# A power's second copy from a DMA to VectorE, three constant loads put back in SyncE's queue, and fewer waits at the program's end

## The chip, the core and the metric

The kernel runs on one core of one Trainium2 chip. The metric is the device time of one execution in microseconds (us), the median of several runs.

## What is computed

The reference mixes two branches over a sequence of 2048 tokens with 512 features, by a gate g of each token:

```python
g = _sigmoid((x * gate_w).sum(-1, keepdims=True))
a = _A_ref(x, A_wq, A_wk, A_wv, A_wo, A_beta)
b = _B_ref(x, B_A_re, B_A_im, B_B_re, B_B_im, B_C_re, B_C_im, B_log_dt, B_Dskip)
return g * a + (1 - g) * b
```

Branch A is causal attention with 32 heads of 16 features, within 4 segments of 512 tokens, plus a read of a memory that collects the earlier segments' keys and values. Branch B is a state space model (S4): from A, B, C and dt it forms a convolution kernel of length 2048 for each of the 512 features,

```python
P = jnp.exp(logdA[:, :, None] * l[None, None, :])
K = jnp.einsum('dn,dnl,dn->dl', Cc, P, dB).real
```

and convolves x with it through Fourier transforms, plus x * Dskip.

## The kernel before

The program is recorded as about 1800 operations, each with an engine, what it reads and writes, and a tag. A table of numbers (ORDER, L375 to L465) gives the sequence in which they are put into the engines' programs, and the buffers that they take; an operation with a number that stands further back is issued later on its engine. Engines run their own programs in order. emit (L267) adds the semaphores: an operation waits only for those earlier operations that its engine does not already know to be done, and this knowledge (know) is passed on through the waits. Each DMA gets a semaphore of its own from a ring of 120.

All DMAs are issued by SyncE (SP), one after the other: loads of inputs and constants, transposes of x, copies from SBUF to SBUF (sb<-sb), stores to the scratch tensors scr_Z and scr_O and loads from them, and 8 stores of the output.

The stages overlap. TensorE (PE) transposes, projects, and multiplies scores; ScalarE (ACT) takes the exponentials of the scores (L1190, L1237) and most evictions from PSUM (L229); VectorE (DVE) builds the tables of the state space kernel, normalises, and applies masks. What the change touches:

- ssm_powers (L840 to L865). For each half h of the features and k from 0 to 9 a complex power z to the 2^k is made by squaring (L850 to L852). A tile pw then holds it in bf16 in four blocks: L857 writes the real and imaginary part (evac of pwc), L862 the negated imaginary part into block 3, and a DMA (L864) copies block 0 into block 1. "Power (3,0)" is k = 3, h = 0. Its copies for k = 2 are not made.
- tables (L1316). For each quarter c it copies powers 0 to 3 into the table F (L1366, which runs as L230 on VectorE), and then multiplies the tables by later powers (L1346, L1349, L1355, L1358). Its fourth copy in quarter 0 reads power (3,0) and waits for the DMA of L864.
- x_level1 (L908). Each of 16 blocks xl1.0 to xl1.15 is multiplied by W1 in two halves, evicted into one of two buffers zs, and stored to scr_Z by a DMA. The next block but one must wait for that store before its eviction.
- Three constant loads: mask01 (32 KB; used by L1249 from 154.5 us on), ones (0.5 KB; used by the product "diag" ahead of L896, at 58.0 us) and sel (6 KB; used in gate_rows, L965, first at 154.3 us).
- The end of SyncE's program (L339 to L342), where it waits for the last count of each of the 120 DMA semaphores. The program's close behind it (L1603) is a barrier of all engines.

Of the kernel before, what the change touches and what calls it, by code (L numbers as in the profile page):

```python
# [98 lines left out]
class Sched:  # L99
# [167 lines left out]
    def emit(self):  # L267
# [43 lines left out]
        cum = {}  # L311
        for e, lst in self.prog.items():
            n = 0
# [10 lines left out]
        def make(e):  # L324
            def run(eng):
                for o in self.prog[e]:
                    need = {}
                    for d in o.waits:
                        s, v = tok(d)
                        if id(s) not in need or need[id(s)][1] < v:  # L330
                            need[id(s)] = (s, v)
                    for s, v in need.values():
                        eng.wait_ge(s, v)
                    ins = o.fn(eng)
                    if o.isdma:
                        ins.then_inc(dsem[o.sem[1]], 16)
                    elif o.inc:
                        ins.then_inc(sems[e], 1)
                if e == "SP":  # L339
                    for k in range(len(dsem)):  # L340
                        if dcnt[k]:
                            eng.wait_ge(dsem[k], 16 * dcnt[k])  # L342
# [21 lines left out]
PW, PWS = (1.0, 8.0), 0.6  # L364
# [16 lines left out]
211a 187/0 212 129/4 1247/0 65 6/0 108 20 127/1 200 128 119 190 1248a 399/0 5/0 183 267a 1036v/0 98v/4 142v/5 213/1/0  # L381
141/6 214a 120 21 139/1 223a 228/0/0/0 1252/2/0 201 229 627/5 628 208/0 1253a 1257/0 140 1040v/0 1039v 1250a 216/3
217a 224 268 1044 225 1037v 1251 1038v 230 842/1 843 130v/6 271/2/1/1 413/1 256/0/0 1042/0 257 1045 151/2 152/7 1254/3
131 1041 153 132 258 231 311/0/2/2 143 1043 89/3 272 233/0/1 234 165/2 227 188 235 1255a 226 154v/7 269/1/1 238/0/2
239 1049 166v/8 312a 144 202/0 1050 270a 155 90 8/0 1237/3/1 156 1046 273 236/0 240 1239/1 1240a 237 241 99/1 1238a
1256 167 242/0/3 168 203/0 243 244 274 1051 1263/2/0 1264a 1047/0 1052 1265/1 101/3 1266a 163/2 357/3/2 287/0/1 288
1053 245 209/0 1048 100 246 1241 416/2 1278/1 289 417a 247/1 1056/0 358a 232/1/0 275 1054 276/0 250/0/3 251 252 400/2
401 1268/3/1 248 164 1270/1 249/0 175a/9 314/2/0 315a 253/0 254 1269a 283/0/3 284 1061 255 259 1055 1271a 1267 4/0 285
1260/2/0 1261a 1272 1258/3 176 177 1057 1259a 278/0/2 279 280 1062 1262 260 261/2 1273/1/1 1275/2 1276a 313 354/3/3/1
355a 316/2/0/0 1274a 1277 1063 301/0/0 1058 262 302 317 1059/0 281/3 263 264 303 403/0 1286/1/0 1287a 282 286 290 402  # L390
291 359/0/1/1 1060 360 319 318 1065 1066/0 295/0/2 292/3 1294/2/1 1295a 296 297 28/0 1067 320/1 361 1296/2 362 363
1068 1069/0 338/0/1 339 1299/0 293 1064 191/0 109/0 1070 1297a 364 1298 192/0 340 1071/2/0 1075/1 1076 1077 204 111/4
110 121/3 294/1 1079/0 1080 1081a 123/0 1072 1078a 205 1073 1074a 1083/0 1086v/0 1088a 1284/3 1285a 1090v/0 122 298/0
356 1087v 299 300 1094 1092/0 1089v 1095 136a/4 330/0/2 331 332 1085 135/6 112v/2 1091 304 1288 133/1 1279/1/1 472/2/1
473a 113 114 1093 305 321/0/3 1099 306/4 1084 1096 322 323 134 145/2 1100 1097/0 1082 405/3/1/0 406a 341/2 342 307
344/0/0 345 1281/3 346 1101 1280a 476/0 308 309 1098 1282a 1283 1102 420/0 1106/0 421a 326/0/1 327 426/1/0/0 146/7 328
1103 1307/3/0 427 1308a 147 157/0 324/0 325 366/0/3 367 368 343 1105 428 408/3/0 1104 80a/0 329 1107 333 334 335/5
# [137 lines left out]
def build_graph(nc, es, A_x, A_wq, A_wk, A_wv, A_wo, A_beta, B_A_re, B_A_im, B_B_re, B_B_im,  # L535
# [304 lines left out]
    def ssm_powers(Zs):  # L840
        Zc = list(Zs)
        for k in range(10):
            for h in range(2):
# [16 lines left out]
                if k == 2:  # L860
                    continue
                op("DVE", ("V4", 256), lambda e, pw=pw: e.tensor_scalar(  # L862
                    ap(pw, 384, [[512, 2], [1, 128]]), ap(pw, 256, [[512, 2], [1, 128]]), -1.0, None, ALU.mult), r=[pw], pw=[pw], key=PW[h] + PWS * k + 0.35)
# [785 lines left out]
```

## Time and profile before

| What | Value |
|---|---|
| Runs of the kernel | 290.23 us median of 3 (289.74, 290.23, 293.19) |
| The profiled execution: span from first to last instruction | 287.5 us |
| Its time outside the span | not recorded; the runs' median is 2.7 us above the span |
| Busy: PE, DVE, ACT | 253.1, 265.0, 254.6 us |
| Mean granted TensorE clock | 0.987 |
| HBM traffic over the span | 104 GB/s |
| Last ACT instruction (L232) ends | 283.0 us |
| Output stores, issue to landing | 8, median 2.1 us |

The profile is of one execution. A row of a timeline gives the start in us from the span's beginning, the length, the engine, line, operation and operands, a count, and in brackets the idle time ahead of it with what ended it; "SPq" rows are DMAs that SyncE issues, and their length is that of the issue. A row of a line ("L225 ... x2: a/b/c, s to e") gives the shortest, median and longest duration in ns, and the first and last start; the landing line under it is the time from issue until the data are there. A row of windows gives the stretch, its length, the busy time of PE, PEld, DVE, ACT and POOL with the number of instructions, the granted clock, the share of the DMA engines, and GB/s.

### The profile page before, as it was taken

What the parts mean: (1) busy time and instruction counts of PE and PEld (TensorE: products, weight loads), DVE (VectorE), ACT (ScalarE), POOL (GpSimd) and SP (SyncE); (2) the same over time, 40 slices, a digit from 0 to 9 for tenths busy, and PEclk for the clock granted to TensorE, in tenths of its full rate; (3) what the DMA queues carried; (4) which work ended last, traced back from release to release, by engine and by line L of the source; (5) the groups of instructions that cost most, each with busy time, mean ns of one, the idle gap of its engine ahead of it and who ended that gap; (6) DMA issues with size and microseconds to landing.
All of it is one profiled execution on the core that took longest, in us unless ns stands there. A gap on an engine that the chain in (4) does not pass through costs nothing.

```text
span 287.5 us, 9336 instructions
## 1 busy us (share of the span) xinstructions
PE 253.1 (88%) x3896; PEld 158.7 (55%) x3947; DVE 265.0 (92%) x617; ACT 254.6 (89%) x320; POOL 5.0 (2%) x10
## 2 busy tenths in 40 slices
PE   5767888787898989979999989999999999999992
PEld 2424454564556546756766657665555454555661
DVE  3998999999999999979999999999999999997782
ACT  5998999999999999989989999999999999983212
POOL 5000000000000000000000000000000000000000
PEclk9999899999999999979999999999999999999999
DMA  6996762421125256914643388585776795894224
GB/s 164 270 223 143 184 203 84 130 87 42 41 47 134 63 141 205 226 32 97 188 132 102 90 252 244 166 232 161 234 215 168 207 229 160 243 186 102 72 109 182
DMA packets 60187, 44.49 MB, mean 155 GB/s; under 512 B 36209, under 2 KB 53490, under 8 KB 60146
## 3 DMA queue, kind: packets, MB, share of 16 engines
q1 hardware_dynamic: 60146, 43.90, 57.0%
q8 instruction: 31, 0.51, 0.8%
q14 instruction: 10, 0.08, 0.1%
HBM read 22.09 MB, written 7.86 MB: 104 GB/s over the span
## 4 chain that ended last, share of the span: by engine, by line
ACT 35%; PE 28%; DVE 26%; issue 5%; DMA 3%; SPq 0%; DVEq 0%; ACTq 0%
PE psum L706 28%; ACT sb L1237 10%; ACT sb L229 10%; ACT sb L1190 8%; DVE sb L1346 7%; DVE sb L1355 3%; ACT sb L850 3%; DVE sb L230 2%; DMA sb<-sb 2%; DVE sb L1349 2%; DVE sb L1487 2%; DVE sb L1358 2%; DVE sb L1249 1%; DVE sb L1154 1%; ACT sb L1021 1%
## 5 line engine op out<-in xcount | busy, mean ns | idle before, releaser
L706 PE MATMUL psum<-sb 128*128 128x17 bf16 (+17 forms) x3808 | 247.4, 229 | 23.5 <-ACT sb L1190 7.4
L706 PEld LDWEIGHTS psum<-sb 128*128 128x128 bf16 (+6 forms) x3859 | 153.5, 102 | 115.5 <-issue 20.7
L229 ACT ACTIVATE sb<-psum 128x512 bf16<-128x512 f32 (+4 forms) x155 | 87.7, 624 | 7.6 <-PE psum L706 6.4
L1237 ACT ACTIVATE sb<-psum 128x2048 bf16<-128x2048 f32 x40 | 76.0, 1899 | 2.1 <-PE psum L706 1.7
L1190 ACT ACTIVATE sb<-psum 128x2048 bf16<-128x2048 f32 (+1 forms) x40 | 70.1, 1751 | 2.8 <-PE psum L706 2.7
L1346 DVE TENSOR_TENSOR sb<-sb 128x4096 bf16<-128x4096 bf16 (+3 forms) x24 | 37.7, 1569 | 0.0
L230 DVE CAST sb<-psum 128x512 bf16<-128x512 f32 (+1 forms) x49 | 29.9, 626 | 1.1 <-PE psum L706 0.9
L1355 DVE TENSOR_TENSOR sb<-sb 128x512 bf16<-128x512 bf16 (+1 forms) x48 | 25.0, 537 | 0.1
L1249 DVE TENSOR_TENSOR sb<-sb 128x1024 bf16<-128x1024 bf16 (+1 forms) x40 | 22.6, 577 | 0.2
L1487 DVE TENSOR_TENSOR sb<-sb 128x1024 bf16<-128x1024 bf16 x32 | 21.6, 685 | 0.9 <-ACT sb L229 0.5
L1349 DVE TENSOR_TENSOR sb<-sb 128x2048 bf16<-128x2048 bf16 (+3 forms) x24 | 20.7, 861 | 0.0
L232 ACT ACTIVATE sb<-psum,sb 128x512 bf16<-128x512 f32 x6 | 4.0, 687 | 12.3 <-PE psum L706 12.3
L1154 DVE TENSOR_TENSOR sb<-psum,sb 128x256 bf16<-128x256 f32 x32 | 13.3, 417 | 0.3
L1358 DVE TENSOR_TENSOR sb<-sb 128x512 bf16<-128x512 bf16 (+1 forms) x24 | 12.9, 536 | 0.0
L850 ACT ACTIVATE sb<-sb 128x512 f32<-128x512 f32 x18 | 11.8, 660 | 0.0
L1151 DVE RECIPROCAL sb<-psum 128x16 f32<-128x16 f32 x32 | 7.9, 252 | 1.8 <-PE psum L706 1.7
L1291 DVE TENSOR_TENSOR sb<-psum,sb 128x512 bf16<-128x512 f32 x12 | 8.2, 687 | 0.2
L858 ACT ACTIVATE sb<-sb 128x512 bf16<-128x512 f32 x12 | 8.0, 683 | 0.0
L1072 ACT ACTIVATE sb<-sb 128x512 bf16<-128x512 bf16 x12 | 8.0, 663 | 0.0
L1021 ACT ACTIVATE sb<-psum 128x512 bf16<-128x512 bf16 x12 | 7.8, 646 | 0.0
L852 DVE SCALAR_TENSOR_TENSOR sb<-sb 128x256 f32<-128x256 f32 x18 | 7.5, 424 | 0.0
L851 DVE TENSOR_TENSOR sb<-sb 128x256 f32<-128x256 f32 x18 | 7.5, 423 | 0.0
(78 smaller groups left out, 122.3 us busy)
## 6 DMA issues: line engine op xcount, KB each, us to landing
sb<-sb SPq DMA_DIRECT2D x64, 128.0 KB, 3.2
sb<-c_DN SPq DMA_DIRECT2D x32, 224.0 KB, 3.0
scr_Z<-sb SPq DMA_DIRECT2D x16, 256.0 KB, 3.2
sb<-scr_Z SPq DMA_DIRECT2D x16, 256.0 KB, 3.6
sb<-in_A_x_dram SPq DMA_DIRECT2D x5, 512.0 KB, 4.6
sb<-c_DN SPq DMA_DIRECT2D x16, 160.0 KB, 3.3
out_dram<-sb SPq DMA_DIRECT2D x8, 256.0 KB, 2.1
scr_O<-sb SPq DMA_DIRECT2D x12, 128.0 KB, 2.7
```

The costliest lines, as they stand in the source:

```text
L229: fa = lambda e: e.activation(dst(), src(), ACT.Copy)
L230: fd = lambda e: e.tensor_copy(dst(), src())
L706: mm = lambda e, o_, l, r_, st, sp, **kw: e.matmul(o_, lhsT=l, rhs=r_, start=st, stop=sp, skip_group_check=True, **kw)
L850: op("ACT", ("As", 512), lambda e, sq=sq, Z=Z: e.activation(ap(sq, n=512), ap(Z, n=512), ACT.Square), r=[Z], w=[sq], key=PW[h] + PWS * k)
L1190: o = op("ACT", ("Ax", 4 * n), lambda e: e.activation(ap(pT, dims=[[512, 4], [1, n]]), ap(P, dims=[[512, 4], [1, n]]), ACT.Exp, scale=0.25 ...
L1237: o = op("ACT", ("Ax", 2048), lambda e, P=P, pT=pT: e.activation(ap(pT, n=2048), ap(P, n=2048), ACT.Exp, scale=0.25), r=[P], w=[pT])
L1249: op("DVE", ("V2", 128 * nb), lambda e, pT=pT, dims=dims: e.tensor_tensor(ap(pT, dims=dims + [[1, 128]]), ap(pT, dims=dims + [[1, 128]]), ...
L1346: op("DVE", ("V2n1" if n == 1 else "V2", 512 * n), lambda e: e.tensor_tensor(ap(tile, 2 * dst, [[2 * (sp - dst), 2], [2 * ne, 128], [1, 2 ...
L1349: op("DVE", ("V2n1" if n == 1 else "V2", 256 * n), lambda e: e.tensor_tensor(D_(), D_(), ap(tile, 2 * sp + ne * 128, [[-ne * 128, 2], [2 * ...
L1355: op("DVE", ("V2x" if sstep > 2 else "V2", 256 * n), lambda e, half=half: e.tensor_tensor(run(t2, n, 0, 1) if half else run(tile, ne, dst, ...
L1358: op("DVE", ("V2", 256 * n), lambda e: e.tensor_tensor(D_(), D_(), ap(t2, n * 128, [[-n * 128, 2], [2 * n, 64], [1, 2 * n]]), ALU.add), r= ...
L1487: op("DVE", ("V2", 1024), lambda e, Y=Y, XAB=XAB, K3=K3, Ke=Ke, xo=xo, u=u: e.tensor_tensor(ap(Y, dims=[[512, 2], [1, 512]]), ap(XAB, xo, ...
```

## The change

Three things are changed.

1. For power (3,0) alone VectorE copies block 0 into block 1, and the DMA that did it is gone. The program has 256 DMAs in place of 257, and the later ones take the semaphore before theirs in the ring.
2. In ORDER the numbers 2/0 (mask01), 6/0 (ones) and 5/0 (sel) stand further back. The numbers themselves keep their meaning, and all others keep their order.
3. At the end of SyncE's program only those DMAs are waited for that no other wait covers. The list is made from the back: a DMA whose count is not yet known to SyncE is put on it, and all that it knows counts as known from then on.

```diff
+        know = last["SP"]
+        tail = []
+        for d in reversed(self.order):
+            if d.isdma and know.get(d.sem, 0) < d.val:
+                tail.insert(0, d)
+                for kk, vv in d.know.items():
+                    if know.get(kk, 0) < vv:
+                        know[kk] = vv
...
                 if e == "SP":
-                    for k in range(len(dsem)):
-                        if dcnt[k]:
-                            eng.wait_ge(dsem[k], 16 * dcnt[k])
+                    for d in tail:
+                        eng.wait_ge(*tok(d))
...
-87 88 106a/2 1242/0 219a 1243a 1245a 104/7 105 115/1 185/0 206/6 107 117/0 91/1 2/0 116 207/0 1246 118a/3 210/1/1/1
+87 88 106a/2 1242/0 219a 1243a 1245a 104/7 105 115/1 185/0 206/6 107 117/0 91/1 116 207/0 1246 118a/3 210/1/1/1 211a
...
                 op("DVE", ("V4", 256), lambda e, pw=pw: e.tensor_scalar(
                     ap(pw, 384, [[512, 2], [1, 128]]), ap(pw, 256, [[512, 2], [1, 128]]), -1.0, None, ALU.mult), r=[pw], pw=[pw], key=PW[h] + PWS * k + 0.35)
+                if (k, h) == (3, 0):
+                    op("DVE", ("V4", 256), lambda e, pw=pw: e.tensor_copy(ap(pw, 128, [[512, 2], [1, 128]]), ap(pw, 0, [[512, 2], [1, 128]])),
+                       r=[pw], pw=[pw], key=PW[h] + PWS * k + 0.4)
+                    continue
                 S.dma(lambda pw=pw: ap(pw, 128, [[512, 2], [1, 128]]), lambda pw=pw: ap(pw, 0, [[512, 2], [1, 128]]), 65536,
                       r=[pw], pw=[pw], key=PW[h] + PWS * k + 0.4)
```

In the rows of the changed program below, line numbers are its own: 7 more than in the profile between L343 and L863, 11 more from L864 on.

SyncE's queue from the second transpose of x on, before. The sb<-sb 128x2x128 copies are second copies of powers: (1,0), then (3,0), then (4,0).

```order
L743 DMA_TRANSPOSE sb<-in_A_x_dram 128x4x512
L225 DMA sb<-sb 128x2x128 [waits q_DVE]
L225 DMA sb<-c_mask01 128x128
L225 DMA scr_Z<-sb 128x2x512 [waits q_ACT]
L225 DMA sb<-c_ones 128x2
L225 DMA sb<-sb 128x2x128 [waits q_DVE]
L743 DMA_TRANSPOSE sb<-in_A_x_dram 128x4x512
L225 DMA sb<-c_sel 128x24
L225 DMA sb<-sb 128x2x128 [waits q_DVE]
L225 DMA sb<-in_A_x_dram 128x2048
```

The same stretch of SyncE's queue now:

```order
L750 DMA_TRANSPOSE sb<-in_A_x_dram 128x4x512
L225 DMA sb<-sb 128x2x128 [waits q_DVE]
L225 DMA scr_Z<-sb 128x2x512 [waits q_ACT]
L750 DMA_TRANSPOSE sb<-in_A_x_dram 128x4x512
L225 DMA sb<-sb 128x2x128 [waits q_DVE]
L225 DMA sb<-in_A_x_dram 128x2048
```

Four DMAs are gone from this stretch: the three loads and the copy of power (3,0); the copies that are left are those of (1,0) and (4,0).

Further back in SyncE's queue, now, around the store of the first attention output to scr_O and the load of Dskip:

```order
L225 DMA sb<-sb 128x2x128 [waits q_DVE]
L225 DMA scr_Z<-sb 128x2x512 [waits q_ACT] x2
L225 DMA sb<-c_mask01 128x128
L225 DMA scr_O<-sb 128x4x128 [waits q_DVE]
L225 DMA sb<-c_sel 128x24
L225 DMA sb<-in_B_Dskip_dram 128x4x1
L225 DMA sb<-in_A_x_dram 128x2048
```

Mask01 and sel have come in here; the other rows stood in this order before. Ones stands between the two, behind the store of xl1.3 and ahead of the copy of power (8,0).

VectorE's program now, from power (3,0)'s negation (its first row) to behind the new copy, which is the row of L872:

```order
L869 TENSOR_SCALAR sb<-sb 128x2x128 [waits q_ACT]
L859 SCALAR_TENSOR_TENSOR sb<-sb 128x256 [waits q_DVE]
L859 SCALAR_TENSOR_TENSOR sb<-sb 128x256
L858 TENSOR_TENSOR sb<-sb 128x256 [waits q_ACT]
L961 TENSOR_SCALAR sb<-psum 128x4 [waits q_PE]
L889 TENSOR_TENSOR sb<-sb 128x512 [waits q_DVE]
L1074 TENSOR_SCALAR sb<-sb 128x512 [waits d19,q_ACT]
L859 SCALAR_TENSOR_TENSOR sb<-sb 128x256 [waits q_DVE]
L872 COPY sb<-sb 128x2x128
L940 TENSOR_SCALAR sb<-sb 128x32
L858 TENSOR_TENSOR sb<-sb 128x256 [waits q_ACT]
L869 TENSOR_SCALAR sb<-sb 128x2x128
```

The copy is the only new row, and it waits for nothing. Further on in the same program, the copies into table F, before:

```order
L230 COPY sb<-sb 128x128x2 [waits q_DVE]
L230 COPY sb<-sb 128x128x2 [waits d25]
L1063 TENSOR_SCALAR sb<-sb 128x512
L1346 TENSOR_TENSOR sb<-sb 128x2x128x2 [waits q_DVE]
L230 COPY sb<-sb 128x128x2 [waits d21]
L230 COPY sb<-sb 128x128x2
```

Now:

```order
L230 COPY sb<-sb 128x128x2 [waits q_DVE]
L230 COPY sb<-sb 128x128x2
L1074 TENSOR_SCALAR sb<-sb 128x512
L1357 TENSOR_TENSOR sb<-sb 128x2x128x2 [waits q_DVE]
L230 COPY sb<-sb 128x128x2 [waits d21]
L230 COPY sb<-sb 128x128x2
```

The second row, which reads power (3,0), no longer waits for a DMA (d25 was the semaphore of its copy).

At the end SyncE waited for all 120 semaphores, in 60 instructions with two semaphores each. Now it waits for six, d13, d14, d12, d15, d11 and d10: those of the last six stores of the output.

More of the change, by code (lines that the diff above doesn't have):

```diff
@@ L379 @@
 189/2 7/0 76 1244/5/0 181/4 1249/4/1 77/3 95/0 22/0 199/0 78/5 96/6 97 103/1 626/0 182/3 86v/1 1/0 184/0 841/0 79 221a
-87 88 106a/2 1242/0 219a 1243a 1245a 104/7 105 115/1 185/0 206/6 107 117/0 91/1 2/0 116 207/0 1246 118a/3 210/1/1/1
-211a 187/0 212 129/4 1247/0 65 6/0 108 20 127/1 200 128 119 190 1248a 399/0 5/0 183 267a 1036v/0 98v/4 142v/5 213/1/0
-141/6 214a 120 21 139/1 223a 228/0/0/0 1252/2/0 201 229 627/5 628 208/0 1253a 1257/0 140 1040v/0 1039v 1250a 216/3
-217a 224 268 1044 225 1037v 1251 1038v 230 842/1 843 130v/6 271/2/1/1 413/1 256/0/0 1042/0 257 1045 151/2 152/7 1254/3
@@ L384 @@
[L384 to L388, printed above, removed]
@@ L389 @@
-1260/2/0 1261a 1272 1258/3 176 177 1057 1259a 278/0/2 279 280 1062 1262 260 261/2 1273/1/1 1275/2 1276a 313 354/3/3/1
[L390 to L397, printed above, removed]
+87 88 106a/2 1242/0 219a 1243a 1245a 104/7 105 115/1 185/0 206/6 107 117/0 91/1 116 207/0 1246 118a/3 210/1/1/1 211a
@@ new lines @@
+187/0 212 129/4 1247/0 65 108 20 127/1 200 128 119 190 1248a 399/0 183 267a 1036v/0 98v/4 142v/5 213/1/0 141/6 214a
+120 21 139/1 223a 228/0/0/0 1252/2/0 201 229 627/5 628 208/0 1253a 1257/0 140 1040v/0 1039v 1250a 216/3 217a 224 268
+1044 225 1037v 1251 1038v 230 842/1 843 130v/6 271/2/1/1 413/1 256/0/0 1042/0 257 1045 151/2 152/7 1254/3 131 1041 153
+132 258 231 311/0/2/2 143 1043 89/3 272 233/0/1 234 165/2 227 188 235 1255a 226 154v/7 269/1/1 238/0/2 239 1049 166v/8
+312a 144 202/0 1050 270a 155 90 8/0 1237/3/1 156 1046 273 236/0 240 1239/1 1240a 237 241 99/1 1238a 1256 6/0 167
@@ new lines @@
+242/0/3 168 203/0 243 244 274 1051 1263/2/0 1264a 1047/0 1052 1265/1 101/3 1266a 163/2 357/3/2 287/0/1 288 1053 245
+209/0 1048 100 246 1241 416/2 1278/1 289 417a 247/1 1056/0 358a 232/1/0 275 1054 276/0 250/0/3 251 252 400/2 401
+1268/3/1 248 164 1270/1 249/0 175a/9 314/2/0 315a 253/0 254 1269a 283/0/3 284 1061 255 259 1055 1271a 1267 4/0 285
+1260/2/0 1261a 1272 1258/3 176 177 1057 1259a 278/0/2 279 280 1062 1262 260 261/2 1273/1/1 1275/2 1276a 313 354/3/3/1
+355a 316/2/0/0 1274a 1277 2/0 1063 301/0/0 1058 262 302 317 1059/0 281/3 263 264 5/0 303 403/0 1286/1/0 1287a 282 286
@@ new lines @@
+290 402 291 359/0/1/1 1060 360 319 318 1065 1066/0 295/0/2 292/3 1294/2/1 1295a 296 297 28/0 1067 320/1 361 1296/2 362
+363 1068 1069/0 338/0/1 339 1299/0 293 1064 191/0 109/0 1070 1297a 364 1298 192/0 340 1071/2/0 1075/1 1076 1077 204
+111/4 110 121/3 294/1 1079/0 1080 1081a 123/0 1072 1078a 205 1073 1074a 1083/0 1086v/0 1088a 1284/3 1285a 1090v/0 122
+298/0 356 1087v 299 300 1094 1092/0 1089v 1095 136a/4 330/0/2 331 332 1085 135/6 112v/2 1091 304 1288 133/1 1279/1/1
+472/2/1 473a 113 114 1093 305 321/0/3 1099 306/4 1084 1096 322 323 134 145/2 1100 1097/0 1082 405/3/1/0 406a 341/2 342
@@ L398 @@
+307 344/0/0 345 1281/3 346 1101 1280a 476/0 308 309 1098 1282a 1283 1102 420/0 1106/0 421a 326/0/1 327 426/1/0/0 146/7
+328 1103 1307/3/0 427 1308a 147 157/0 324/0 325 366/0/3 367 368 343 1105 428 408/3/0 1104 80a/0 329 1107 333 334 335/5
 1108 375/0/1 376 347 160a/3 377 348 1109/0 349/0 418/1 371/0/2 372 419a 409a 1111 124a/1 373 1110 469/1/0/2 1302/3/1
```

## The prediction

> **What bounds the kernel now.** I read the page first, then the chain that ended last, then the timelines of the engines around the two places that the change touches (20 to 31 us, and the end), and last the rows of single transfers.
>
> The page's head, its busy times and the chain's shares by engine:
>
> ```profile
> span 287.5 us, 9336 instructions
> PE 253.1 (88%) x3896; PEld 158.7 (55%) x3947; DVE 265.0 (92%) x617; ACT 254.6 (89%) x320; POOL 5.0 (2%) x10
> ACT 35%; PE 28%; DVE 26%; issue 5%; DMA 3%; SPq 0%; DVEq 0%; ACTq 0%
> ```
>
> No engine is the bound by itself: three are busy for 88 to 92% of the span and share the chain. A stall that holds two of them at once is therefore likely to reach the end, and work that is taken off one of them alone is not. The chain holds one such stall early; these are its pieces from 22 to 31 us (start, length, what):
>
> ```profile
> 22.87 3.02 DMA sb<-sb
> ...
> 25.92 0.30 DVE sb L230
> ...
> 27.63 2.99 PE psum L706 x16
> ...
> 30.64 1.88 ACT sb L1190
> ```
>
> The transfer at 22.87 is the second copy of power (3,0): the vector engine's L230 behind it starts when it lands. What each engine sees of it, first VectorE (start, length, what, and in brackets the idle time before it with its releaser):
>
> ```profile
> 18.79 0.23 DVE L862 TENSOR_SCALAR sb<-sb 128x256 bf16<-128x256 bf16 x1
> ...
> 21.65 0.22 DVE L862 TENSOR_SCALAR sb<-sb 128x256 bf16<-128x256 bf16 x1
> 21.79 0.42 DVE L885 SCALAR_TENSOR_TENSOR sb<-sb 128x256 bf16<-128x256 f32 x1
> ...
> 25.92 0.30 DVE L230 COPY sb<-sb 128x256 bf16<-128x256 bf16 x1 [1.43 <-DMA sb<-sb]
> ```
>
> L862 at 18.79 is the negation that completes power (3,0), so its copy could have been issued at about 19.0. It was issued at 22.87, because SyncE's queue stood in the way:
>
> ```profile
> 20.47 0.61 SPq L225 DMA_DIRECT2D sb<-c_mask  x1
> 21.12 1.20 SPq L225 DMA_DIRECT2D scr_Z<-sb  x1
> 22.36 0.47 SPq L225 DMA_DIRECT2D sb<-c_ones  x1
> 22.87 0.95 SPq L225 DMA_DIRECT2D sb<-sb  x1
> 23.87 2.04 SPq L743 DMA_TRANSPOSE sb<-in_A_x_dram  x1
> 25.95 0.57 SPq L225 DMA_DIRECT2D sb<-c_sel  x1
> 26.58 0.61 SPq L225 DMA_DIRECT2D sb<-sb  x1
> ```
>
> These follow each other within 0.06 us: the queue is the limit here, and three of its seven entries are the loads that the change puts back, a fourth the copy that it removes.
>
> ScalarE and TensorE have a stall of their own at the same time:
>
> ```profile
> 25.39 1.58 ACT L229 ACTIVATE sb<-psum 128x512 bf16<-128x512 f32 x3 [1.14 <-DMA scr_Z<-sb]
> ...
> 30.64 1.88 ACT L1190 ACTIVATE sb<-psum 128x2048 bf16<-128x2048 f32 x1 [0.39 <-PE psum L706]
> ```
>
> ```profile
> 26.04 0.40 PE L1018 MATMUL psum<-sb 128*128 128x128 bf16 x4 [1.63 <-ACT sb L229]
> ...
> 27.63 4.02 PE L706 MATMUL psum<-sb 128*128 128x512 bf16 x20 [0.37 <-DVE sb L1022]
> ```
>
> ScalarE waits for the store of xl1.1 to the scratch tensor (a buffer of two that its next eviction needs), TensorE for that eviction. So all three engines stand still near 25 us, for two transfers out of one queue.
>
> **The change part by part.** *VectorE's copy.* It adds one instruction of 256 bf16 values a partition. No row shows this copy; L862 with the same pattern is the nearest: it occupies the engine for 0.14 us (21.65 to 21.79) and takes 0.22 in all. I take 0.14, since nothing in the order waits for it directly behind. It stands where VectorE has no idle time, so it costs its full length. It removes the 1.43 us wait, so at 26 us VectorE is 1.43 - 0.14 = 1.29 us earlier. What would be late next is the landing of power (4,0), whose issue stands at 26.58: with mask, ones, the copy and sel gone from ahead of it (0.65 + 0.51 + 1.00 + 0.63 = 2.79 us, from start to start in the rows), it starts near 23.8. VectorE first uses it here:
>
> ```profile
> 31.35 0.70 DVE L1346 TENSOR_TENSOR sb<-sb 128x1024 bf16<-128x1024 bf16 x1
> ```
>
> That would be at 31.35 - 1.29 = 30.06, and even a landing that takes 4.2 us, as the scratch store's below, comes at 28.0 and leaves no wait.
>
> *The mask load ahead of the scratch store.* The store of xl1.1 starts up to 0.65 us earlier (21.12 - 20.47). Its landing:
>
> ```profile
> L225 SPq DMA_DIRECT2D scr_Z<-sb x1: 1196/1196/1196, 21.1 to 21.1; - x1
> ...
> DMA to landing us min/median/max: 4.2/4.2/4.2
> ```
>
> 21.12 + 4.2 = 25.3 is where ScalarE's wait ends. The gain is 0.65 us if the store keeps its 4.2, and nothing if it was held by the transfers already in flight; below nothing would need a new transfer ahead of it, and the order puts none there. I take 0.65, because the mask's own 32 KB also leave the transfers in front of it. ScalarE's other wait there, 0.39 at 30.64, hangs on TensorE's 2.99 us of work behind 27.63, which also starts earlier (its 0.37 wait was for VectorE), and which ran at half clock:
>
> ```profile
> 28.00:29.00 1.00, 1.00 (x4) 0.30 (x2) 1.00 (x4) 1.00 (x1) 0.00 (x0) 0.50 0.62 91
> ```
>
> The columns behind the length are the engines' busy times; the clock is the third last, 0.50. This window follows the idle 1.63 us at 24.4 to 26.0, and that idle time shrinks with ScalarE's wait. If the window runs at full clock, ScalarE's 0.39 goes too: 0.65 to 1.04 us for ScalarE, against 1.29 for VectorE. The Trainium skill, page "TensorE: Matmul & The Clock Gate", section "HAM oscillation — how this bites in real kernels", puts the rule otherwise: only idle gaps of more than about 3.4 us bring the clock down. The trace disagrees, 1.63 us were followed by 0.50. By the page a shorter gap would change no clock, and the early gain would be 0.65 and the time 287.7.
>
> What of this reaches the end? VectorE and ScalarE have few idle stretches after 31 us:
>
> ```profile
> 76.14 0.26 DVE L1151 RECIPROCAL sb<-psum 128x16 f32<-128x16 f32 x1 [0.33 <-PE psum L706]
> ...
> 125.02 0.29 DVE L230 COPY sb<-sb 128x256 bf16<-128x256 bf16 x1 [1.07 <-PE psum L706]
> ```
>
> Between 31 and 124 us no wait of VectorE's is longer than the first of these. Everything later waits for other engines and not for a fixed time, so a shift of all three engines passes through; the one that shifts least may hold the others. Between 0.65 and 1.29 I take 1.0. The ends kept for the range are 0 and 1.3.
>
> *The loads at their new places.* Ones now stands behind the fourth scratch store, ahead of power (8,0)'s copy: 0.5 us there, against 2.8 us by which the queue is ahead. Mask and sel come around 52 us:
>
> ```profile
> 48.07 3.60 SPq L225 DMA_DIRECT2D scr_Z<-sb  x2
> 52.53 0.38 SPq L225 DMA_DIRECT2D scr_O<-sb  x1
> 52.95 0.51 SPq L225 DMA_DIRECT2D sb<-in_B_Dskip_dram  x1
> ```
>
> ```profile
> L896 DVE TENSOR_TENSOR sb<-psum,sb x1: 162/162/162, 58.0 to 58.0; 128x4 f32<-128x4 f32 x1
> ```
>
> Between the scratch stores' end (51.67) and the store to scr_O the queue is free for 0.86 us, and mask fits in with 0.61. Sel delays the load of Dskip by about 0.6, and L896 needs Dskip at 58.0, or 57.0 when all is 1.0 earlier. It did not wait there before, so the load took at most 58.0 - 52.95 = 5.05 us; then it would land at 52.95 - 1.0 + 0.6 + 5.05 = 57.6, and VectorE would wait 0.6. The page gives the like load of gate_w, with 1 KB in pieces of two bytes:
>
> ```profile
> sb<-in_gate_w_dram SPq DMA_DIRECT2D x1, 1.0 KB, 5.9
> ```
>
> That one shared the queue with 0.5 MB loads, and 5.9 is over the 5.05 that is possible here. I take nothing, and 0.6 as a loss for the range. Ones is used by the product ahead of L896, so near 57 us, and mask first here (sel in the same stretch), so that none of the three is waited for:
>
> ```profile
> L1249 DVE TENSOR_TENSOR sb<-sb x40: 365/682/693, 154.5 to 259.4; 128x1024 bf16<-128x1024 bf16 x24, 128x512 bf16<-128x512 bf16 x16
> ```
>
> *The waits at the end.* The rows of the waits, of the last two stores, and of one us with what the transfers moved (last column GB/s):
>
> ```profile
> L342 SPq EVENT_SEMAPHORE  x60: 17/28/28, 283.4 to 287.0; - x60
> ```
>
> ```profile
> L225 SPq DMA_DIRECT2D out_dram<-sb x2: 333/333/333, 281.8 to 283.0; - x2
> ...
> DMA to landing us min/median/max: 2.0/2.0/2.1
> ```
>
> ```profile
> 285.00:286.00 1.00, 0.00 (x0) 0.00 (x0) 0.00 (x0) 0.00 (x0) 0.00 (x0) 1.00 0.00 0
> ```
>
> The last store is issued at 283.0 and lands at 283.0 + 2.0 = 285.0; from then on nothing moves. But SyncE goes on through its 60 wait instructions, two semaphores in each, until 287.0: (287.0 - 283.4) / 59 = 0.061 us each. They are slow because they are many, not because they wait. With three left (six semaphores), SyncE is through them by 285.0 + 2 x 0.061 = 285.1, and the close that now takes from 287.06 to 287.5 follows: end at 285.6, a gain of 1.9 us. The ends: 2.1 if only the landing counts (287.06 - 285.0), and 0.9 if the last store lands as slowly as 3.0 us, which is what the early copy took (22.87 to 25.9). I take 1.9, because stores to the output took 2.0 in both rows. The cover of the other waits is their users': each is waited for by an engine that works on before the end.
>
> **The sum.** 1.9 + 1.0 = 2.9 us: span 287.5 - 2.9 = 284.6. The profiled execution shows its span alone; the runs' median of 290.23 is 2.7 above it, which I leave as it is: 290.2 - 2.9 = 287.3 us.
>
> **The rivals.**
> - *Only the end counts.* If the 1.0 us is swallowed, because an engine that has gained less holds the others, or the scratch store lands no earlier, the time is 290.2 - 1.9 = 288.3. For it speaks that three engines share the chain, against it that the chain itself runs through the copy.
> - *The end's waits are hidden anyway.* Were the 3.6 us a wait for a landing, three instructions would end as late as sixty, and only the early 1.0 would come: 289.2. The even pitch and the transfers' silence from 285 us on speak against it.
> - *The clock gives more.* There is a second half-clock window, and the chain runs through TensorE there:
>
> ```profile
> 123.00:126.40 3.40, 1.74 (x43) 1.32 (x37) 2.33 (x9) 2.61 (x4) 0.00 (x0) 1.00 0.03 7
> 126.40:129.80 3.40, 3.40 (x42) 2.69 (x41) 3.02 (x10) 2.83 (x3) 0.00 (x0) 0.50 0.23 51
> ```
>
>   It follows 3.4 us in which TensorE was busy for 1.74. Moving the work by 1 us against the windows could make it miss: 3.4 / 2 = 1.7 us more, 285.6.
> - *Slower, through the clock.* The same mechanism the other way: half-clock windows that are not there now. Each costs at most 1.7 us, where TensorE carries the chain. One is not enough (289.0); from the second on the kernel is slower than before, 287.3 + 3.4 = 290.7. It would need new stretches in which TensorE works for about half of 3.4 us, and the change makes the known one shorter.
>
> **How the numbers follow.** The forecast, both terms in some size, gets 0.52; only the end 0.24; more by the clock 0.10; the end hidden 0.07; slower 0.04; 0.03 is for what I don't see. The likeliest gives 287.3. Its smallest and largest terms are 0.9 + 0 - 0.6 (289.9) and 2.1 + 1.3 (286.8); the range reaches to the clock's case below and, short of the least likely sums, to 289.3 above: 285.4 to 289.3, which leaves out less than 2 in 10. Two per cent, about what a measurement of this kernel can tell from no change, is 5.8 us. Faster than 284.4 needs the clock's case and more, 0.07; slower than 296.0 needs six new windows (8.7 / 1.7), or what I don't see, 0.03; within 2%: 0.90.
>
> **What would show it.** In the profile of the changed kernel VectorE's wait of 1.43 us for the sb to sb transfer is gone, and no other of more than 0.3 us stands before 31 us; ScalarE's wait for the scratch store is 0.5 us or less; the clock near 28 us tells whether the window was missed. Three waits are left at the end, and the span ends 0.6 us or so behind the last landing. L896 has no idle time ahead of it. I am wrong if ScalarE's wait stays at 1.1 us, if a new wait for a later power or for Dskip stands on VectorE, or if the end comes more than 1 us behind the last landing.

## The result and the profile after

The changed kernel's median is 287.37 us (285.84 to 290.85, 11 runs), the first kernel's beside it 289.93 us (287.97 to 293.19, 11 runs). The ratio is 0.9898, with a 95% interval of 0.9865 to 0.9931: 3.0 us less (2.0 to 3.9), against a forecast of 2.9. A repeat (e8_whole below, with runs of the first kernel of its own) gave 2.0 us (0.6 to 3.3). The two terms of the forecast did not fare alike, though: the end gave what was forecast, the early part gave little or nothing.

The page's head of the changed kernel, its busy times and the chain's shares by engine:

```profile
span 285.5 us, 9331 instructions
PE 259.6 (91%) x3947; PEld 157.9 (55%) x3947; DVE 265.2 (93%) x618; ACT 254.8 (89%) x320; POOL 5.0 (2%) x10
PE 45%; ACT 44%; DMA 4%; issue 3%; DVE 1%; SPq 0%; ACTq 0%; DVEq 0%
```

VectorE has one instruction more and SyncE far fewer; the span is 2.0 us shorter. Two of these numbers can't be compared with those of before. PE's 51 more matmuls are records that the first profile lacks (the weight loads are 3947 in both), so PE's busy time has not grown by 6.5 us. And VectorE's share of the chain, 26% before and 1% now, is not the early part's doing: e2_early and e7_ahead below, with the same early code, have 28% and 23%; the share is 1 to 9% in the four profiles with all 3947 matmul records and 10 to 28% in the ten others.

**The end.** The last two stores of the changed kernel, their landing, and the close (SyncE's closing branch):

```profile
L225 SPq DMA_DIRECT2D out_dram<-sb x2: 332/332/332, 281.7 to 283.0; - x2
...
DMA to landing us min/median/max: 2.0/2.0/2.1
```

```profile
L349 SPq EVENT_SEMAPHORE  x3: 17/27/28, 283.4 to 285.0; - x3
```

```profile
L1614 SPq COMPARE_BRANCH  x1: 41/41/41, 285.1 to 285.1; - x1
```

The last store is issued at 283.0, as in the profile before, and lands 2.0 us later, at 285.0. Now the last of three waits also stands at 285.0, where it stood at 287.0 as the last of sixty, and the span ends 0.5 us behind it. This repeats in every profile: the span ends 2.4 to 2.6 us behind the last landing in the six kernels with the old end and single waits (the first, e2_early, e3_copy, e4_loads, e6_late, e12_before_pool), and 0.5 in the seven with the new one.

**The early part.** VectorE, ScalarE and TensorE where the three stalls were:

```profile
24.34 0.41 DVE L858 TENSOR_TENSOR sb<-sb 128x256 f32<-128x256 f32 x1
24.67 0.43 DVE L230 COPY sb<-sb 128x256 bf16<-128x256 bf16 x2
24.94 0.35 DVE L1074 TENSOR_SCALAR sb<-sb 128x512 bf16<-128x512 bf16 x1
```

```profile
24.64 1.58 ACT L229 ACTIVATE sb<-psum 128x512 bf16<-128x512 f32 x3
29.36 1.91 ACT L1201 ACTIVATE sb<-psum 128x2048 bf16<-128x2048 f32 x1
```

```profile
25.29 0.40 PE L1029 MATMUL psum<-sb 128*128 128x128 bf16 x4 [0.55 <-ACT sb L229]
```

No bracket of idle time is left on VectorE or ScalarE (1.43 and 1.14 us before), and TensorE's 1.63 us is 0.55. ScalarE's L1201 starts at 29.36, where the same instruction (then L1190) started at 30.64: 1.3 us earlier. So at 30 us the forecast's 1.0 is there, and more. But the clock's window at half speed came elsewhere (columns as in the windows shown before; the third last is the clock):

```profile
30.00:31.00 1.00, 0.14 (x1) 0.00 (x0) 1.00 (x3) 1.00 (x1) 0.00 (x0) 0.99 0.62 159
31.00:32.00 1.00, 0.68 (x34) 0.56 (x35) 1.00 (x5) 1.00 (x3) 0.00 (x0) 0.50 0.64 147
32.00:37.00 5.00, 5.00 (x50) 2.81 (x49) 5.00 (x10) 4.55 (x7) 0.00 (x0) 0.50 0.46 133
37.90:45.00 7.10, 6.74 (x139) 4.48 (x138) 6.21 (x13) 6.98 (x10) 0.00 (x0) 1.00 0.37 102
```

28 us now runs at full clock, but 31.0 to 37.8 at half (6.8 us). ScalarE's lead (the start of an instruction here less that of the same instruction before) is 1.3 us at 31 us, 0.3 at 60 and none at 75; it comes back to 1.8 at 130, where the first kernel's profiled execution has a half-clock window at 126.4 and this one has none; and at 214 it is 0.2. Of the 2.0 us between these two spans nothing is thus left to the early part.

### The profile page after: what moved, and what is told of

It is laid out like the page before. It is cut to its first block, busy times and chain, and to the rows that moved or that the text cites. A ratio compares the mean times of both kernels' runs of the same rounds, so it can differ in the third digit from the quotient of the medians.

```text
span 285.5 us, 9331 instructions
## 1 busy us (share of the span) xinstructions
PE 259.6 (91%) x3947; PEld 157.9 (55%) x3947; DVE 265.2 (93%) x618; ACT 254.8 (89%) x320; POOL 5.0 (2%) x10
## 4 chain that ended last, share of the span: by engine, by line
PE 45%; ACT 44%; DMA 4%; issue 3%; DVE 1%; SPq 0%; ACTq 0%; DVEq 0%
PE psum L713 45%; ACT sb L1201 15%; ACT sb L229 13%; ACT sb L1248 8%; ACT sb L857 3%; DMA sb<-scr_Z 2%; ACT sb L865 2%; DMA sb<-c_DN 2%; ACT sb L1032 1%; DMA sb<-c_ident 1%; ACT sb L1083 1%; ACT L939 0%; SPq L225 0%; PE psum L1029 0%; DVE sb L817 0%
## 5 line engine op out<-in xcount | busy, mean ns | idle before, releaser
L713 PE MATMUL psum<-sb 128*128 128x17 bf16 (+18 forms) x3859 | 254.2, 231 | 17.7 <-ACT sb L1201 7.7
L1201 ACT ACTIVATE sb<-psum 128x2048 bf16<-128x2048 f32 (+1 forms) x40 | 69.8, 1744 | 2.6 <-PE psum L713 2.3
L1498 DVE TENSOR_TENSOR sb<-sb 128x1024 bf16<-128x1024 bf16 x32 | 21.6, 684 | 0.9 <-ACT sb L229 0.5
```

Of the source, the lines that this page charges most:

```text
L713: mm = lambda e, o_, l, r_, st, sp, **kw: e.matmul(o_, lhsT=l, rhs=r_, start=st, stop=sp, skip_group_check=True, **kw)
L1201: o = op("ACT", ("Ax", 4 * n), lambda e: e.activation(ap(pT, dims=[[512, 4], [1, n]]), ap(P, dims=[[512, 4], [1, n]]), ACT.Exp, scale=0.25 ...
L1498: op("DVE", ("V2", 1024), lambda e, Y=Y, XAB=XAB, K3=K3, Ke=Ke, xo=xo, u=u: e.tensor_tensor(ap(Y, dims=[[512, 2], [1, 512]]), ap(XAB, xo, ...
```

## The experiments

Twelve kernels were run. Where a ratio is given, it is to the first kernel on the same chip.

### The end alone, and the early part alone

e1_tail is the first kernel with the change of emit only:

```diff
-                    for k in range(len(dsem)):
-                        if dcnt[k]:
-                            eng.wait_ge(dsem[k], 16 * dcnt[k])
+                    for d in tail:
+                        eng.wait_ge(*tok(d))
```

> The kernel before with the change at the end alone: six semaphores waited for instead of 120; the copy stays a DMA and the three loads stay where they were. If the two terms add up as forecast: 1.9 us faster than before (0.9 to 2.1), and VectorE's 1.43 us and ScalarE's 1.14 us waits near 25 us are still there. If only the end counts, it is as fast as the whole change, near 2.6 us faster. If the end's waits are hidden behind the last landing: no change. In the profile the end should come 0.5 us behind the last landing, against 2.5 us before.

e2_early has the copy and the moved loads, and the old end (the whole diffs of both stand with the change):

```diff
+                if (k, h) == (3, 0):
...
-87 88 106a/2 1242/0 219a 1243a 1245a 104/7 105 115/1 185/0 206/6 107 117/0 91/1 2/0 116 207/0 1246 118a/3 210/1/1/1
+87 88 106a/2 1242/0 219a 1243a 1245a 104/7 105 115/1 185/0 206/6 107 117/0 91/1 116 207/0 1246 118a/3 210/1/1/1 211a
```

> The early part alone: VectorE's copy and the three loads put back, with the 120 waits at the end as before. As forecast: 1.0 us faster (0 to 1.3). If only the end counts: no change. If the end is hidden: all of the gain, near 2.6 us. Five rounds tell about 1 us, so the profile counts beside the time: by the forecast every engine runs 1 us or so ahead of before all the way to the last store; by the rival the lead is there at 30 us and gone later, at a wait that can be named.

e3_copy has VectorE's copy alone (the first hunk of e2_early), e4_loads the moved loads alone (the second).

> VectorE's copy alone, loads and end as before. The mask load still stands ahead of the store of xl1.1, so ScalarE's wait of 1.1 us at 25 us stays while VectorE's of 1.43 goes. If the shift of the engine that gains least is what counts: 0 to 0.3 us faster. If VectorE's shift alone counts: 1.3 us faster. If only the end counts: no change.

> The three loads put back alone; the copy is a DMA, the end as before. The copy is issued 1.2 us earlier (mask 0.65 and ones 0.51 are gone from ahead of it), so VectorE's wait shrinks from 1.43 to about 0.3, and ScalarE's from 1.14 to about 0.5. As forecast: 0.7 us faster, nearly what the whole early part gives. If only the end counts: no change.

| Kernel | Ratio, 95% interval | In us | Span of its profile |
|---|---|---|---|
| e1_tail | 0.9932 (0.9898 to 0.9966) | -2.0 (-2.9 to -1.0) | 284.9 |
| e2_early | 1.0015 (0.9980 to 1.0049) | +0.4 (-0.6 to +1.4) | 287.3 |
| e3_copy | 0.9999 (0.9962 to 1.0036) | 0.0 (-1.1 to +1.0) | 286.0 |
| e4_loads | 1.0001 (0.9972 to 1.0030) | 0.0 (-0.8 to +0.9) | 286.1 |

The end alone is worth 2.0 us, the forecast's 1.9. The early part alone is worth nothing that these runs can show: a gain of 1.0 lies outside e2_early's interval. The two parts of it are no better one by one. Their profiles did not all look as expected. In e3_copy, and in e9_tail_copy below, ScalarE's wait of 1.1 us for the scratch store was to stay, as mask's load still stands ahead of that store; neither trace has it. In e4_loads, and in e10_tail_loads below, VectorE's wait for power (3,0) was to shrink to 0.3 us, and it is gone.

### The whole, and the end with each early part

e8_whole is the changed kernel again, e9_tail_copy the end with VectorE's copy, e10_tail_loads the end with the moved loads; their diffs are sums of those above. The question was whether an early part works only once the end is short.

> The whole change again, on one chip with the two kernels below, since the early part alone gave no gain (1.5 per mille slower, interval 2.0 per mille faster to 4.9 slower) where the forecast had 1.0 us faster. If the early part gives what the stall is on average (VectorE's wait was 1.43, 0.79 and 0.29 us in the three profiles with the early code of before, 0.84 in the mean, less 0.14 for the copy): 1.9 + 0.7 = 2.6 us faster than before. If it gives nothing: 1.9 us, as the end alone (0.9932).

> The change at the end and VectorE's copy, with the three loads where they were before. VectorE's wait is gone, ScalarE's for the scratch store stays (1.14, 0.45 and under 0.15 us in the three profiles with the old early code). If the stall's mean counts: 2.2 to 2.6 us faster than before. If the early part gives nothing: 1.9.

> The change at the end and the three loads put back, with the copy as a DMA. The copy is issued about 1.2 us earlier and VectorE's wait should be gone or under 0.3. If the stall's mean counts: 2.4 to 2.6 us faster than before, as much as the whole change. If the early part gives nothing: 1.9.

| Kernel | Ratio, 95% interval | In us | Span of its profile |
|---|---|---|---|
| e8_whole | 0.9932 (0.9884 to 0.9979) | -2.0 (-3.3 to -0.6) | 285.4 |
| e9_tail_copy | 0.9946 (0.9904 to 0.9988) | -1.6 (-2.8 to -0.3) | 284.1 |
| e10_tail_loads | 0.9934 (0.9899 to 0.9970) | -1.9 (-2.9 to -0.9) | 286.5 |

All three are the end's 2.0 within their intervals. The first comparison's 3.0 (2.0 to 3.9) stands at its upper side; the early part may hold some tenths of a us, not 1.0 and more.

### Is it the number of waits, and their place?

e5_twice is the first kernel with every semaphore waited for twice, e7_ahead the changed kernel with a wait for every semaphore put ahead of the first output store, where SyncE's queue is empty:

```diff
-                    for k in range(len(dsem)):
+                    for k in list(range(len(dsem))) * 2:
```

```diff
+                    if o.isdma and o.tag[:3] == "out" and not any(p.tag[:3] == "out" for p in self.prog[e][:o.idx - 1]):
+                        seen = {}
+                        for p in self.prog[e][:o.idx - 1]:
+                            seen[p.sem[1]] = p.val
+                        for k in sorted(seen):
+                            eng.wait_ge(dsem[k], 16 * seen[k])
```

> The kernel before, with each of the 120 semaphores waited for twice at the end: 120 wait instructions in place of 60. If the price is in the instructions (0.061 us each): 60 x 0.061 = 3.7 us slower. If the end only waits for the last landing: no change, since all have landed by then.

> The changed kernel with waits for all semaphores put back, but ahead of the first output store, where the queue's engine waits for some 8 us anyway; behind the last store only the six waits stand. If the cost of the waits is their place behind the last store: as fast as the changed kernel (2.6 us faster than before). If the instructions cost wherever they stand: 3.6 us slower than the changed kernel, 1 us slower than before.

The waits of e5_twice, then those of e7_ahead (instructions, shortest, median and longest in ns, first and last start):

```profile
L342 SPq EVENT_SEMAPHORE  x120: 17/28/28, 282.6 to 290.9; - x120
```

```profile
L345 SPq EVENT_SEMAPHORE  x59: 27/28/28, 268.0 to 271.5; - x59
```

```profile
L355 SPq EVENT_SEMAPHORE  x3: 17/28/28, 284.1 to 285.7; - x3
```

e5_twice: ratio 1.0183 (1.0134 to 1.0232), 5.3 us more (3.9 to 6.7); the 3.7 expected lies just outside. Its 120 instructions take 8.3 us, of which 0.7 is a wait for the last landing and 0.4 a gap. Its span ends 7.1 us behind the last landing (284.2), where the first kernel's ends 2.4 behind its own (285.0): 4.7 us more, which is the 3.7 of 60 instructions, the wait and the gap, and lies inside the runs' interval. What makes the gap the trace doesn't tell. (Its span of 291.3 is only 3.8 over the first kernel's because this execution issued its last store 0.8 us earlier, at 282.2.) e7_ahead: 0.9934 (0.9900 to 0.9968), 1.9 us less. The same 59 waits take 3.5 us there too, (271.5 - 268.0) / 58 = 0.060 each, and cost nothing. So it is in the main the count of instructions behind the last store that is paid for, and not what they wait for: the rival by which the end was hidden anyway is out.

### Does an early stall reach the end?

e6_late is the first kernel with the copy of power (3,0), number 108 in ORDER, moved behind a transpose of x and the load of sel, to stand directly ahead of power (4,0)'s copy (120):

```diff
-211a 187/0 212 129/4 1247/0 65 6/0 108 20 127/1 200 128 119 190 1248a 399/0 5/0 183 267a 1036v/0 98v/4 142v/5 213/1/0
-141/6 214a 120 21 139/1 223a 228/0/0/0 1252/2/0 201 229 627/5 628 208/0 1253a 1257/0 140 1040v/0 1039v 1250a 216/3
+211a 187/0 212 129/4 1247/0 65 6/0 20 127/1 200 128 119 190 1248a 399/0 5/0 183 267a 1036v/0 98v/4 142v/5 213/1/0
+141/6 214a 108 120 21 139/1 223a 228/0/0/0 1252/2/0 201 229 627/5 628 208/0 1253a 1257/0 140 1040v/0 1039v 1250a 216/3
```

> The kernel before with the copy of power (3,0) put further back in the DMA queue, behind the transpose of x and the load of sel, just ahead of the copy of power (4,0). It is issued about 3.1 us later (where the load of power (4,0) stood, 26.0), lands near 28.5 or 29, and VectorE's wait of 1.43 us grows to 4 or 4.5. If an early stall passes to the end in full: 2.5 to 3 us slower. If later waits swallow it, as the rival for the early part has it: under 1 us slower.

Ratio 1.0118 (1.0079 to 1.0157), 3.4 us more (2.3 to 4.5). VectorE's copy into F and TensorE's product behind it:

```profile
28.60 0.30 DVE L230 COPY sb<-sb 128x256 bf16<-128x256 bf16 x1 [3.46 <-DMA sb<-sb]
```

```profile
30.31 2.97 PE L706 MATMUL psum<-sb 128*128 128x512 bf16 x16 [3.48 <-DVE sb L1022]
```

VectorE's wait is 3.46 us, less than the 4 to 4.5 expected. ScalarE is 2.7 us late at 31 us and still 2.7 late at 60; at 130 and at 230 us it is 1.0 and 1.1 late, but it is compared there with an execution that has a half-clock window at 126.4, as this one has not. That the stall is passed on in full therefore rests on the times: 3.4 us more (2.3 to 4.5) for a wait that has grown by 2.0 us over the first kernel's profile, or by 2.8 over the mean of the executions below. So a stall here is on the path, as forecast. This rules out that the early stall was off the critical path; the gain must have been smaller than forecast, or lost further on.

### How large the stall is, and where a lead goes

The first kernel's early code also runs in e1_tail, e5_twice and e12_before_pool (below). VectorE's copy of power (3,0) into F in e1_tail, e5_twice and e12_before_pool (there in one group with the copy ahead of it, without a wait):

```profile
25.55 0.30 DVE L230 COPY sb<-sb 128x256 bf16<-128x256 bf16 x1 [0.79 <-DMA sb<-sb]
```

```profile
25.64 0.30 DVE L230 COPY sb<-sb 128x256 bf16<-128x256 bf16 x1 [0.29 <-DMA sb<-sb]
```

```profile
25.06 0.47 DVE L230 COPY sb<-sb 128x256 bf16<-128x256 bf16 x2
```

The wait was 1.43, 0.79, 0.29 and 0 us in four executions of the same code: 0.63 in the mean. The profile that I forecast from had the longest of them. ScalarE's wait for the scratch store scatters as well: 1.14 in the first kernel, 0.45 in e1_tail, none in e5_twice and e12_before_pool; and in e11_whole_pool, which has the moved loads, it is back (below). Over all fourteen profiles (of the first kernel, the changed one and these twelve) it stands in two of the seven that have mask's load ahead of the store, and in one of the seven that have not. So the 0.65 us that the forecast took for this store can't be laid to mask's load by these traces.

```profile
25.20 1.58 ACT L229 ACTIVATE sb<-psum 128x512 bf16<-128x512 f32 x3 [0.89 <-DMA scr_Z<-sb]
```

This table gives ScalarE's lead in each profiled execution (the start of an instruction less that of the same one in the first kernel's profile; minus is earlier), and the half-clock windows ahead of the last matmul:

| Kernel | 31 us | 60 us | 75 us | 130 us | 180 us | 230 us | Half clock from (us), length |
|---|---|---|---|---|---|---|---|
| first kernel | 0 | 0 | 0 | 0 | 0 | 0 | 27.4, 126.4 (3.4 each) |
| e1_tail | -1.1 | -0.7 | +0.4 | -1.5 | -1.5 | -0.6 | 62.2 (3.4) |
| e5_twice | -0.8 | -0.1 | 0.0 | -1.9 | -1.6 | -0.8 | 19.7 (3.4) |
| e12_before_pool | -0.7 | -0.6 | -0.2 | -0.2 | -0.1 | +0.6 | 19.6, 125.4 (3.4 each) |
| changed kernel | -1.3 | -0.3 | +0.1 | -1.8 | -1.4 | -0.2 | 31.0 (6.8) |
| e2_early | -1.3 | -1.2 | +0.2 | -0.5 | -0.4 | -0.2 | 18.2, 62.6 (3.4 each) |
| e7_ahead | -1.1 | -1.1 | 0.0 | -0.1 | +0.5 | +0.6 | 18.8, 63.2, 124.6 (3.4 each) |
| e8_whole | -1.2 | -1.1 | -0.7 | -2.1 | -2.0 | -0.2 | 18.8 (3.4) |
| e11_whole_pool | -0.7 | -0.1 | +1.0 | -0.9 | +0.2 | +1.3 | 34.7, 62.0 (3.4 each) |

The first four have the old early code, the other five the new one. Their means at 31 us are -0.65 and -1.12: 0.5 us apart, and not 1.0 to 1.3. At 230 us they are -0.2 and +0.3, so none of it is to be seen there; but the single values at 230 us lie up to 2.1 us apart, and means of four and five of them can't tell a gain of 0.5 us from none. Two things stand between. The first is the clock. Every execution with a window near 62 us loses 1.1 us or more between 60 and 75 us, and every one with a window near 125 us lacks the 0.7 to 1.9 us that the others gain there on the first kernel, which has one at 126.4. In e1_tail:

```profile
62.60:65.60 3.00, 2.77 (x27) 1.31 (x28) 1.57 (x6) 2.94 (x3) 0.00 (x0) 0.50 0.49 137
```

The places of these windows are not quite chance. In all fourteen traces the clock changes on a grid of 3.413 us alone, and the grid stands elsewhere in each execution. Of its stretches at full clock from 8 us to the end of the products, all 8 in which TensorE was busy for at most 0.48 of the time were followed by half clock, 15 of the 95 with 0.49 to 0.74, and none of the 961 with more. Those that were followed by it begin at 14 to 17, 24 to 31, 59 to 60 and 121 to 123 us, where TensorE stands idle for a large part of the time; as far as these traces tell, which of these places loses its clock goes by how the grid falls on it.

The second is SyncE's queue and its transfers between 185 and 215 us. Of this table, the executions that come there 1.4 to 2.0 us early lose 0.8 to 1.8 of it, while e2_early and e7_ahead, which come 0.4 early and 0.5 late, lose 0.1 to 0.2. But that they lose it because they come early is not shown. e3_copy and e4_loads came 2.1 and 2.0 early and lost 0.6, e9_tail_copy came 1.7 early and lost 0.3; e12_before_pool came 0.1 early and lost 0.7, e10_tail_loads 0.5 early and lost 1.5, and e11_whole_pool 0.2 late and lost 1.1. What goes with the loss is the longest wait of VectorE or TensorE for a landing there: none over 0.25 us in the first kernel, e2_early and e6_late, which lost 0 to 0.3; 0.3 to 0.5 in e7_ahead, e3_copy and e9_tail_copy, which lost 0.1 to 0.6; 0.8 to 1.9 in the eight others, which lost 0.6 to 1.9. The first kernel's profile, from which all leads are counted, happened to have no such wait, so that nearly every other execution seems to lose there. The longest such waits are e8_whole's. There SyncE issues without a gap from 184 to 197 us, and all three engines then wait for what it brings; first VectorE (L1498 is the product with the spectra, one of whose operands is a copy from SBUF to SBUF) and TensorE, then pieces of the chain of waits:

```profile
200.22 0.69 DVE L1498 TENSOR_TENSOR sb<-sb 128x1024 bf16<-128x1024 bf16 x1 [1.86 <-DMA sb<-sb]
```

```profile
200.13 14.16 PE L713 MATMUL psum<-sb 128*128 128x256 bf16 x145 [1.45 <-DMA sb<-c_DN]
```

```profile
194.47 5.52 DMA sb<-c_DN
199.99 0.14 issue
200.13 3.98 PE psum L713 x35
```

In the first kernel's profile no engine waits for a DMA between 194 and 214 us. In the changed kernel's own profile it is a load from scr_Z that held TensorE at 209.75, 1.04 us long; the load had taken 5.72 us to land, where the median of its kind is 3.7.

### Relief for the queue at 185 us

Would the early gain come out at the end if the queue there were shorter? e11_whole_pool is the changed kernel with seven of the loads of c_DN on GpSimd's queue, e12_before_pool the first kernel with the same edit:

```diff
-            S.dma(lambda CD=CD: ap(CD, n=896), lambda u=u: hC[u], 229376, w=[CD], key=kx - 6)
+            S.dma(lambda CD=CD: ap(CD, n=896), lambda u=u: hC[u], 229376, w=[CD], key=kx - 6, q="POOL" if 10 <= u < 17 else "SP")
```

> The changed kernel with seven of the 32 loads of c_DN (the eleventh to the seventeenth, which SyncE issues between 187 and 204 us) issued by GpSimd's queue instead. Nothing is left out. Theory A, the early lead is given back in this stage: every profiled execution whose engines were 1.4 to 2.1 us ahead of the first kernel's at 180 us lost 0.2 to 1.9 us of it by 214 us, while those that were not ahead lost 0.1 to 0.2; there SyncE's queue runs without a gap and the loads of c_DN land late. With seven entries less the waits for c_DN and for sb from sb between 196 and 210 us stay under 0.3 us on every engine, ScalarE's lead at 214 us equals that at 180 us within 0.3, and the ratio to the first kernel falls from 0.993 by about 1.0 us to 0.990. Theory B, these waits are scatter of single landings and the rest is the clock's windows: the ratio stays at 0.993. Theory C, the loads start later through GpSimd's queue than through SyncE's: a wait for c_DN of more than 0.5 us on TensorE, ratio 0.995 or above.

> The first kernel with the same seven loads of c_DN issued by GpSimd's queue. Nothing is left out. Theory A: the first kernel's own executions that come early to 180 us are held there too (the one with doubled waits lost 0.8 us), so it gains about half of what the changed kernel gains by the same edit, 0.5 us, ratio 0.998. Theory B: 1.000. Theory C: 1.002 or above.

e11_whole_pool: 0.9927 (0.9897 to 0.9958), 2.1 us less; e12_before_pool: 1.0027 (1.0002 to 1.0052), 0.8 us more. Neither gained. The edit did not do what it was meant to: the loads are not queued in the order of u, so GpSimd issued only one of the seven between 184 and 200 us, and SyncE's copies behind it still held its queue without a gap until 202.6:

```profile
195.55 7.05 SPq L225 DMA_DIRECT2D sb<-sb  x5
```

TensorE waited again, 1.20 us for a load from scr_Z at 211.5. None of the three theories is settled by it: e11_whole_pool's time stayed where theory B had it, e12_before_pool's went where theory C had it (1.002 or above), though from 180 us on TensorE has no wait for c_DN in either trace; and the stretch was not relieved. Whether a shorter queue at 185 us would let the lead through stays open.

## Why the prediction held, and where it did not

- **The end, 1.9 us.** Right in mechanism and size: 2.0 us alone (1.0 to 2.9). The even pitch of the waits and the silence of the transfers, on which it rested, were the right rows: 59 satisfied waits take the same 0.06 us each where they add nothing to the time (e7_ahead), and 60 more at the end move the span's end 4.7 us further behind the last landing and add 5.3 us (3.9 to 6.7) to the time (e5_twice). The bound of 0.9, by a slow last store, did not come: it landed in 2.0 us in every profile. The 2.7 us between the first kernel's median and its profiled span, which the sum carries along, are not the time outside the span: where a run's time and span are both on record, the time is 1.7 to 2.2 us longer. The forecast doesn't hang on it, as both terms are differences.
- **VectorE's copy.** Right in the rows: its wait is gone and no other stands before 31 us. That the copy at 0.14 us lay in a full stretch cost nothing that shows (e3_copy 0.0).
- **The loads at their new places.** Right: mask's issue in front of the store to scr_O took 1.51 us and not 0.61, but no engine waits for it, for ones, sel or Dskip. The 0.6 us that I kept as a loss did not come.
- **The clock near 28 us.** The window at 27.4 was missed, as I thought possible, but not because the idle stretch had shrunk: in the changed kernel's profile the 3.4 us from 27.6 on have TensorE busy for 0.47 of the time, with a wait of 0.96 us and most of one of 1.18 for ScalarE, and half clock follows at 31.0. The windows stand in other places from one execution to the next, with either code.
- **The early gain, 1.0 us.** This is the term that was mis-sized, within the range that I kept for it (0 to 1.3). "Between 0.65 and 1.29 I take 1.0": the runs give -0.4 (a loss, e2_early; a gain of at most 0.6), 0.0 and 0.0 alone, and none over the end in e8_whole. Two steps of its working failed. The first was to take both stalls from one profiled execution as what the code costs: the four executions of the same code show 1.43, 0.79, 0.29 and 0 for VectorE's, and ScalarE's is there or away with either order of the loads; the code's gain at 31 us is about 0.5. The second was "a shift of all three engines passes through". A delay does (e6_late); a lead meets half-clock windows worth 0.7 to 1.9 us each, which come or stay away from one execution to the next, and a stretch at 185 to 215 us in which most executions waited for a late landing. As far as the windows don't depend on the code they are noise, which the runs average out; they hide a gain of some tenths and don't remove it. The stretch at 185 us would remove it if an early execution waits there longer than a late one, which is not shown. So the mis-sized stall is shown, and where the last half us went stays open.
- **The rivals.** "Only the end counts" (288.3, a chance of 0.24) is what the experiments say, for a reason that I had put more narrowly. That the total still fell on the likeliest case's 287.3 is luck, as far as the runs tell: that comparison's 3.0 stands a us above the 2.0 of the repeat and of the end alone, with overlapping intervals, and most of the us lies in the first kernel, whose 289.93 there is over the 287.85 to 288.84 of its four other sets of runs, while the changed kernel's 287.37 is near its repeat's 287.04. (The four sets are from different chips, so this comparison is a rough one.) "The end's waits are hidden anyway" is ruled out. "The clock gives more" and "slower, through the clock" took the windows for a property of the code; both happen, from one execution to the next.

## What to carry to other kernels

What stands behind the last transfer is paid for by the instruction: count the waits at the program's end, and keep only those that nothing else covers, or put them where the queue is idle. A stall in one profiled execution is one draw: before it is put into a sum, look for the same instruction in a second execution, above all if a DMA's landing ends it. In this kernel, whose engines are all busy at 90%, a delay early on of 2 to 3 us reached the end, but a gain of some tenths could not be seen there. A gain may meet each later place where transfers were just in time, so look up the smallest margin after it and not only the waits that are there; that it is lost at such a place is not shown here.

## What the runs showed of the hardware

- A wait instruction of SyncE whose semaphores are long satisfied takes 0.06 us: 0.061 at the end of the first kernel, 0.060 at 268.0 to 271.5 us in e7_ahead.
- The half-clock windows last 3.4 us or twice that. They begin at 18 to 20, 27 to 35, 62 to 63 and 125 to 126 us, at some of these places in one execution and at others in the next, with the same code. One at the last two places moves the work that follows by 0.7 to 1.9 us. In the fourteen traces TensorE was busy for 0.02 to 0.74 of the 3.4 us ahead of each. The Trainium skill, page "TensorE: Matmul & The Clock Gate", section "What's actually happening", says that the gate looks at windows of 3413 ns which run freely and don't start with the kernel. The lengths agree with it, 3.4 and 6.8 us; so does the distance of the first kernel's two windows, 126.4 - 27.4 = 99.0 us or 29.0 times 3.413.
- The landing of one and the same kind of load scatters: in the changed kernel's profile 3.7 us in the median for 256 KB from scr_Z, and 5.72 us for the one that held TensorE.
